# Hashed attention and a SwiGLU block: hash products in four 32-column tiles, a first pair loaded in halves, and a bank of its own for the sums

## The chip, the cores and the metric

The kernel runs on one core of a Trainium2 chip. The metric is the device time of one launch in microseconds (us), median of several runs. "Before" measured 1153.05 us in its first three runs (1152.74 to 1157.72).

PE is TensorE, DVE is VectorE, ACT is ScalarE, POOL is GpSimd and SP is SyncE, which issues most transfers. In profile lines, L248 is line 248 of that kernel's own file, so the same statement has another number in another kernel: hash products are L248 before and L276 (full width) or L285 (packed) after. The names in them: qraw and kraw are the loaded q and k, tps the transposes and qT and kT their copies, hps the hash products, qb and kb the bits, sc the scores, A their exponentials, acc the running sums of A, av the products of A with v, e and r parts of the softmax's division, g and val the two first products of the feed-forward, t and ht what is made of them, words the weights as they arrive.

## The reference, cut to what matters

```python
# q, k, v: (4, 8, 768, 64); proj: (64, 6)
q_bits = einsum('bhsd,dk->bhsk', q, proj) > 0      # 6 bits per row; k_bits alike
mask   = bucket(q_bits)[:, :, :, None] == bucket(k_bits)[:, :, None, :]
attn   = softmax(where(mask, q @ k.T / 8, -1e9))
x      = (attn @ v)                                 # as (3072, 512)
out    = (silu(x @ w_gate) * (x @ w_val)) @ w_out   # 512 -> 1536 -> 512
```

The weights arrive as float64 words and are narrowed to float32 on VectorE.

## The kernel before

Two heads form a pair (128 partitions); 4 batches of 4 pairs make 16. A pair is worked in 12 units (two halves of q, six chunks of k), two units to a loop step. During batch one TensorE has only attention; from batch two on it works the feed-forward of the batch before, cut into "atoms", between the attention steps. Meanwhile the next pair is prepared: q and k are transposed, by TensorE in the first five pairs and by VectorE later, multiplied with the hash weights, and the signs become the bits.

```python
def front_bank(name):                # where transposes and hash products land
    return side_bank(name) if atoms or next(turn) % 3 == 2 else bank(name)
# side_bank: one bank, shared with the softmax sums; bank: two, shared with the feed-forward

def hash_bits(name, half):
    ...
    ps = front_bank("hps")
    nc.tensor.matmul(ps[:, 0:HQ], hash_w[name], T[name, n][:, cols], start=True, stop=True)
    if name == "q":
        nc.scalar.activation(o, ps[:, 0:HQ], AF.Sign, bias=nudge)
    else:
        nc.vector.tensor_scalar(o, ps[:, 0:HQ], scalar1=above_k, scalar2=times_k,
                                op0=ALU.is_gt, op1=ALU.mult)
...
for half in range(2):                # order: q0, k0, q1, k1
    for name in "qk":
        steps.append(lambda name=name, half=half: hash_bits(name, half))
...
# per loop step: two scores, the sums that are due, two attends, then:
while atoms and credit >= 1.0:       # about three atoms
    atoms.pop(0)()
    narrow_on(4)                     # four VectorE instructions on the weights
    if mine: mine.pop(0)()           # a step of the next pair
```

The softmax here doesn't subtract the row's maximum and nothing guards it: scores larger than these inputs give would overflow.

## Time and profile before

| What | Before | How to read it |
|---|---|---|
| time | 1153.05 us | median of runs |
| TensorE busy | 99% | union of its instructions |
| hash products on TensorE | 64, in 128 records | a float32 product is two records, called its two passes here |
| start to start of one hash product | 0.65 us | from the timeline in the second half |
| TensorE idle for VectorE's softmax sums | 5.5 us | all of it in batch one |

The lines that carry this stand in the prediction. The evacuation of the hash products, per instruction (line, operation, out and in, count | busy us, mean ns | idle before and its releaser), in the page of before:

```profile
L253 DVE TENSOR_SCALAR kb<-hps,above_k,times_k 128x384 bf16<-128x384 f32 x32 | 21.6, 674 | 57.7 <-PE hps L248 57.0
L251 ACT ACTIVATE qb<-hps,nudge 128x384 bf16<-128x384 f32 x32 | 18.6, 581 | 61.0 <-PE hps L248 61.0
```

### The profile page before, as it was taken

How to read it: one execution, taken by the hardware profiler on the slowest of the kernel's cores; microseconds unless marked ns; L12 is line 12 of the kernel's file. 1: busy time of each engine (PE TensorE's matmuls, PEld its weight loads, DVE VectorE, ACT ScalarE, POOL GpSimd, SP SyncE). 2: the span in 40 equal slices, each digit the busy share in tenths (PEclk: the TensorE clock that was granted, in tenths of full speed). 3: DMA queues.
4: the chain of work that ended last, by engine and by line, in shares of the span. 5: the costliest groups of instructions: out<-in, count | busy, mean ns of one | idle time of the engine just before them, and what ended most of it. 6: DMA issues, size and time to landing. Idle time of an engine off the chain costs nothing.

```text
span 1152.5 us, 10719 instructions
## 1 busy us (share of the span) xinstructions
PE 1139.5 (99%) x4357; PEld 562.2 (49%) x4357; DVE 527.4 (46%) x783; ACT 260.9 (23%) x397; POOL 19.5 (2%) x46
## 2 busy tenths in 40 slices
PE   8999999999999999999999999999999999999998
PEld 4444455555444455555544445555554445555543
DVE  4898999999931244334432143443433222222100
ACT  4544221211212212222221222222222120101000
POOL 0000000000000000000000000000000000000000
PEclk9999999999999999999999999999999999999999
DMA  6332424223110220200002040010000000000000
GB/s 146 78 96 60 104 79 119 74 98 102 62 33 19 50 37 1 42 1 14 1 12 48 19 81 7 11 31 1 14 1 10 19 19 9 1 1 0 1 28 28
DMA packets 97874, 44.74 MB, mean 39 GB/s; under 512 B 86048, under 2 KB 90144, under 8 KB 97824
## 3 DMA queue, kind: packets, MB, share of 16 engines
q1 hardware_dynamic: 91200, 25.83, 10.0%
q0 software_dynamic: 4896, 17.83, 4.9%
q8 instruction: 34, 0.56, 0.2%
q10 hardware_dynamic: 1728, 0.40, 0.2%
q14 instruction: 16, 0.13, 0.0%
HBM read 37.75 MB, written 6.29 MB: 38 GB/s over the span
## 4 chain that ended last, share of the span: by engine, by line
PE 98%; DVE 1%; DMA 0%; ACT 0%; SPq 0%; issue 0%; ACTq 0%
PE g L341 22%; PE po L362 22%; PE val L341 22%; PE sc L288 14%; PE av L299 11%; PE hps L248 4%; PE sum L320 2%; DVE r L323 1%; PE tps L238 1%; DMA qraw<-in_q_dram 0%; ACT A L290 0%; DVE wv L205 0%; SPq L100 0%; ACT o L366 0%; DVE t L348 0%
## 5 line engine op out<-in xcount | busy, mean ns | idle before, releaser
L341 PE MATMUL val<-xT,wv 128*128 128x384 f32 x768 | 266.1, 489 | 0.3 <-DVE wv L205 0.3
L341 PE MATMUL g<-xT,wg 128*128 128x384 f32 x768 | 265.9, 489 | 0.0
L362 PE MATMUL po<-wo,ht 128*128 128x512 f32 x576 | 255.4, 596 | 0.0
L290 ACT ACTIVATE A<-sc 128x768 f32<-128x768 f32 x192 | 155.4, 813 | 204.0 <-PE sc L288 196.0
L341 PEld LDWEIGHTS val<-xT,wv 128*128 128x128 f32 x768 | 143.9, 190 | 110.5 <-DVE acc L307 6.0
L341 PEld LDWEIGHTS g<-xT,wg 128*128 128x128 f32 x768 | 143.9, 190 | 109.8 <-DVE acc L307 6.0
L362 PEld LDWEIGHTS po<-wo,ht 128*128 128x128 f32 x576 | 107.5, 190 | 138.4 <-issue 134.9
L288 PE MATMUL sc<-qT,kT 64*128 64x384 f32 x768 | 155.1, 482 | 0.0
L323 DVE RECIPROCAL r<-sum 128x384 f32<-128x384 f32 x32 | 81.8, 2557 | 149.4 <-PE sum L320 149.4
L299 PE MATMUL av<-A,vraw 128*64 128x386 f32 x768 | 144.1, 496 | 0.0
L347 ACT ACTIVATE t<-g 128x384 f32<-128x384 f32 x96 | 47.1, 491 | 415.9 <-PE g L341 415.9
L348 DVE SCALAR_TENSOR_TENSOR t<-t,g 128x384 f32<-128x384 f32 x96 | 53.0, 552 | 191.7 <-ACT t L347 191.7
L307 DVE TENSOR_TENSOR acc<-acc,A 128x768 f32<-128x768 f32 x128 | 122.2, 955 | 33.7 <-ACT A L290 28.7
L353 DVE SCALAR_TENSOR_TENSOR ht<-t,val 128x384 f32<-128x384 f32 x96 | 53.0, 552 | 114.3 <-PE val L341 114.3
L299 PEld LDWEIGHTS av<-A,vraw 128*64 128x64 f32 x768 | 49.3, 136 | 81.4 <-issue 80.1
L288 PEld LDWEIGHTS sc<-qT,kT 64*128 64x128 f32 x768 | 68.7, 189 | 21.4 <-issue 21.4
L288 PE MATMUL sc<-qb,kb 64*128 64x384 bf16 x384 | 63.6, 328 | 0.1
L288 PEld LDWEIGHTS <-kb 64*128 64x128 bf16 x384 | 18.7, 93 | 67.9 <-issue 54.6
L366 ACT COPY o<-po 128x512 f32<-128x512 f32 x24 | 14.1, 586 | 159.7 <-PE po L362 159.7
L253 DVE TENSOR_SCALAR kb<-hps,above_k,times_k 128x384 bf16<-128x384 f32 x32 | 21.6, 674 | 57.7 <-PE hps L248 57.0
L251 ACT ACTIVATE qb<-hps,nudge 128x384 bf16<-128x384 f32 x32 | 18.6, 581 | 61.0 <-PE hps L248 61.0
L303 DVE SCALAR_TENSOR_TENSOR acc<-A 128x768 f32<-128x768 f32 x32 | 30.5, 952 | 0.5 <-ACT A L290 0.5
(65 smaller groups left out, 373.7 us busy)
## 6 DMA issues: line engine op xcount, KB each, us to landing
vraw<-in_v_dram SPq DMA_DIRECT2D x16, 384.0 KB, 3.5
words<-in_moe_w_val_dram POOLq DMA_DIRECT2D x12, 512.0 KB, 3.8
words<-in_moe_w_out_dram POOLq DMA_DIRECT2D x12, 512.0 KB, 3.5
out_dram<-o SPq DMA_DIRECT2D x24, 256.0 KB, 2.0
words<-in_moe_w_gate_dram POOLq DMA_DIRECT2D x10, 512.0 KB, 4.0
qraw<-in_q_dram SPq DMA_DIRECT2D x44, 96.0 KB, 3.4
kraw<-in_k_dram SPq DMA_DIRECT2D x44, 96.0 KB, 3.0
qraw<-in_q_dram SPq DMA_DIRECT2D x10, 192.0 KB, 5.4
```

What stands on the lines that cost most here:

```text
L248: nc.tensor.matmul(ps[:, 0:HQ], hash_w[name], T[name, n][:, cols], start=True, stop=True)
L288: nc.tensor.matmul(sc[:, h, 0:HQ], x["k", n][rows, ks], x["q", n][rows, qs], start=start, stop=not start)
L290: nc.scalar.activation(ring[u % RING][:, :, 0:HQ], sc[:, :, 0:HQ], AF.Exp, scale=SCALE)
L299: nc.tensor.matmul(ps[h * D : (h + 1) * D, 0:AW], raws["v", n][:, h, c, :], a[:, h, :], start=c == 0, stop=c == NCH - 1)
L303: nc.vector.scalar_tensor_tensor(out=acc[n, half], in0=ring[(u - 1) % RING][:, :, 0:HQ], scalar=S * EPS / P, in1=a[:, :, 0:HQ], op0=ALU.ad ...
L307: nc.vector.tensor_tensor(acc[n, half], acc[n, half], a[:, :, 0:HQ], op=ALU.add)
L323: nc.vector.reciprocal(r, ps[:, 0:HQ])
L341: nc.tensor.matmul(ps[:, 0:HQ], w[:, j, f * P : (f + 1) * P], x[:, j, half * HQ : (half + 1) * HQ], start=j == 0, stop=j == NJ - 1)
L347: nc.scalar.activation(t, ps[:, 0:HQ], AF.Tanh, scale=0.5)
L348: nc.vector.scalar_tensor_tensor(out=t, in0=t, scalar=1.0, in1=ps[:, 0:HQ], op0=ALU.add, op1=ALU.mult)
L353: nc.vector.scalar_tensor_tensor(out=ht, in0=now["t"], scalar=0.5, in1=ps[:, 0:HQ], op0=ALU.mult, op1=ALU.mult)
L362: nc.tensor.matmul(ps, hs[half][f][:, i * P : (i + 1) * P], wo[:, f, :], start=f == 0, stop=f == NF - 1)
```

## The change

The intent is to cut TensorE's work and its idle time. A hash product needs only 26 of its 128 output columns. With both heads' columns inside one group of 32, the four products of a pair (q and k, two halves each) fit side by side in four 32-column tiles, and land in one bank, 32 partitions each. From the ninth pair on this is done. Each quarter is then copied to two 32-row places by two instructions. The sums keep a bank to themselves in batch one. The first pair's q and k come in halves, so that scores can begin after half of the preparation. Other edits come with it: q and k have one raw buffer instead of two, the second pair's loads go behind the first weights, and the second halves are hashed in the order k, q instead of q, k.

```diff
 def front_bank(name):
-    return side_bank(name) if atoms or next(turn) % 3 == 2 else bank(name)
+    return side_bank(name) if atoms else bank(name)

+def hash_blocks():
+    ps = front_bank("hps")
+    where = [(name, half) for name in "kq" for half in range(2)]
+    for i, (name, half) in enumerate(where):
+        nc.tensor.matmul(ps[i * BLOCK : (i + 1) * BLOCK, 0:HQ], hash_w[name][:, 0:BLOCK],
+                         T[name, n][:, half * HQ : (half + 1) * HQ], start=True, stop=True)
+    for i, (name, half) in enumerate(where):
+        for to in (0, D):
+            sign(name, half, slice(to, to + BLOCK), ps, slice(i * BLOCK, (i + 1) * BLOCK))
 ...
-for half in range(2):
-    for name in "qk":
-        steps.append(lambda name=name, half=half: hash_bits(name, half))
+if n >= 2 * NP:
+    return steps + [hash_blocks]
+order = [("q", 0), ("k", 0), ("k", 1), ("q", 1)]
+# first pair: q0 k0 before the first score, then k1, then q1, each transposed and hashed
 ...
-load(0, nc.scalar)                    # whole q, k, v; two raw buffers
+fetch(0, "q", nc.sync, 0)             # first half of q; one raw buffer for q and for k
+fetch(0, "k", nc.scalar, 0)
+fetch(0, "k", nc.sync, 1)
+fetch(0, "v", nc.sync)
+fetch(0, "q", nc.sync, 1)
 ...
-load(1)                               # then the first two pieces of the weights
+load_words(0, nc.sync); load_words(1, nc.sync); load(1)
-    if at == 0 and n + 1 < len(pairs):
+    if at == (4 if n == 0 else 0) and n + 1 < len(pairs):
```

(Cut: the set-up of the hash weights and of the three constant columns, which follows the new layout.)

More of the change, by code (lines that the diff above doesn't have):

```diff
@@ L79, with fetch @@
     raws = {}
-    def load(n, k_queue=nc.sync):
+    def fetch(n, name, queue, half=None):
         b, pr = pairs[n]
-        for name, src, queue in (("q", q, nc.sync), ("k", k, k_queue)):
-            t = raw.tile([P, NCH, 2, D], FP32, tag=name + "raw", name=name + "raw")
-            if n > NP:
-                blocks = t.rearrange("p c a b -> p (c a b)").rearrange(
-                    "p (c a d) -> p c a d", a=P // BLOCK, d=BLOCK)
-                for h in range(2):
-                    for x in range(D // BLOCK):
-                        at = h * D + x * BLOCK
-                        queue.dma_start(
-                            blocks[at : at + BLOCK],
-                            src[b, 2 * pr + h][:, x * BLOCK : (x + 1) * BLOCK].rearrange(
-                                "(a p c) d -> p c a d", c=NCH, p=BLOCK))
-                raws[name, n] = t
-                continue
-            for h in range(2):
-                queue.dma_start(t[:, :, h, :],
-                                  src[b, 2 * pr + h].rearrange("(p c) d -> p c d", c=NCH))
-            raws[name, n] = t
-        t = raw.tile([P, 2, NCH, D], FP32, tag="vraw", name="vraw")
-        nc.sync.dma_start(
-            t.rearrange("p h c d -> p h (c d)"),
-            v[b, 2 * pr : 2 * pr + 2].rearrange("h (p c) d -> p h (c d)", c=NCH),
-        )
-        raws["v", n] = t
@@ L110 @@
-    load(0, nc.scalar)
+        if name == "v":
+            t = raws["v", n] = raw.tile([P, 2, NCH, D], FP32, tag="vraw", name="vraw")
+            queue.dma_start(
+                t.rearrange("p h c d -> p h (c d)"),
+                v[b, 2 * pr : 2 * pr + 2].rearrange("h (p c) d -> p h (c d)", c=NCH),
+            )
+            return
+        src = q if name == "q" else k
+        if not half:
+            raws[name, n] = raw.tile([P, NCH, 2, D], FP32, tag=name + "raw", name=name + "raw",
+                                     bufs=1)
@@ new lines, in fetch @@
+        t = raws[name, n]
+        if n <= NP:
+            cs = slice(None) if half is None else slice(half * CH, (half + 1) * CH)
+            for h in range(2):
+                queue.dma_start(t[:, cs, h, :],
+                                src[b, 2 * pr + h].rearrange("(p c) d -> p c d", c=NCH)[:, cs, :])
+            return
+        blocks = t.rearrange("p c a b -> p (c a b)").rearrange(
+            "p (c a d) -> p c a d", a=P // BLOCK, d=BLOCK)
+        for h in range(2):
+            for x in range(D // BLOCK):
+                at = h * D + x * BLOCK
+                queue.dma_start(
+                    blocks[at : at + BLOCK],
+                    src[b, 2 * pr + h][:, x * BLOCK : (x + 1) * BLOCK].rearrange(
+                        "(a p c) d -> p c a d", c=NCH, p=BLOCK))
@@ L112, with load @@
+    def load(n):
+        for name in "qkv":
+            fetch(n, name, nc.sync)
+    two_proj = konst.tile([P, NBITS], FP32, tag="proj", name="proj")
+    for o in (0, D):
+        nc.gpsimd.dma_start(two_proj[o : o + D, :], proj[:, :])
+    fetch(0, "q", nc.sync, 0)
[3 more added lines that the diff above has]
+    fetch(0, "q", nc.sync, 1)
     ident = konst.tile([P, P], FP32, tag="ident", name="ident")
@@ L120 @@
         nc.tensor.matmul(ps, zeros[:, 0:P], zeros, start=True, stop=True)
-    two_proj = konst.tile([P, NBITS], FP32, tag="proj", name="proj")
-    for o in (0, D):
-        nc.scalar.dma_start(two_proj[o : o + D, :], proj[:, :])
+    HR = 16
+    assert 2 * NBITS + 1 <= HR and 2 * HR == BLOCK
+    rules = konst.tile([P, 3, P], FP32, tag="rules", name="rules")
+    nc.gpsimd.memset(rules[:, 0, :], -(2.0**-120))
+    nc.gpsimd.memset(rules[:, 1:3, :], 0.0)
+    groups = rules.rearrange("p x (g r) -> p x g r", r=HR)
+    nc.gpsimd.memset(groups[:, 0, :, 2 * NBITS : 2 * NBITS + 1], 1.0)
+    nc.gpsimd.memset(groups[:, 1, :, NBITS : 2 * NBITS + 1], -1.0)
+    for h in range(2):
+        g = groups[:, 2, h * D // HR + h, :]
+        nc.gpsimd.memset(g[:, 0:NBITS], OFF)
+        nc.gpsimd.memset(g[:, NBITS : 2 * NBITS], -OFF / 2)
+        nc.gpsimd.memset(g[:, 2 * NBITS : 2 * NBITS + 1], -NBITS * OFF / 2)
+    nc.vector.tensor_tensor(rules, rules, ident.unsqueeze(1).to_broadcast([P, 3, P]), op=ALU.mult)
+    columns = konst.tile([P, 3], FP32, tag="columns", name="columns")
+    nc.vector.tensor_reduce(out=columns, in_=rules, axis=AX.X, op=ALU.add)
+    nudge, above_k, times_k = (columns[:, x : x + 1] for x in range(3))
     hash_w = {}
@@ L130 @@
         hash_w[name] = konst.tile([P, P], FP32, tag="hash" + name, name="hash" + name)
-        nc.gpsimd.memset(hash_w[name], 0.0)
-    def column(name, first, second, third, rest):
-        t = konst.tile([P, 1], FP32, tag=name, name=name)
-        nc.vector.memset(t, rest)
-        for o in (0, D):
-            nc.vector.memset(t[o : o + 2 * NBITS + 1], third)
-            nc.vector.memset(t[o : o + 2 * NBITS], second)
-            nc.vector.memset(t[o : o + NBITS], first)
-        return t
-    nudge = column("nudge", -1e-37, -1e-37, 1.0, -1e-37)
-    above_k = column("above_k", 0.0, -1.0, -1.0, 0.0)
-    times_k = column("times_k", OFF, -OFF / 2, -NBITS * OFF / 2, 0.0)
-    ones = konst.tile([P, D], FP32, tag="ones", name="ones")
-    nc.vector.memset(ones, 1.0)
-    for name in "qk":
-        for o in (0, D):
-            for at in (0, NBITS) if name == "q" else (0,):
-                nc.vector.tensor_copy(hash_w[name][o : o + D, o + at : o + at + NBITS],
-                                      two_proj[o : o + D, :])
+        nc.vector.memset(hash_w[name], 0.0)
+        for h in range(2):
+            rows = slice(h * D, (h + 1) * D)
+            for at in (0, NBITS) if name == "q" else (0,):
+                at += h * HR
+                nc.vector.tensor_copy(hash_w[name][rows, at : at + NBITS], two_proj[rows, :])
+        nc.vector.tensor_copy(hash_w[name][:, D : D + BLOCK], hash_w[name][:, 0:BLOCK])
+    sides = {}
+    for name in "qk":
+        for i in range(2):
+            sides[name, i] = konst.tile([P, S], BF16, tag=name + f"b{i}", name=name + "b")
+    ones = konst.tile([P, D], FP32, tag="ones", name="ones")
+    nc.gpsimd.memset(ones, 1.0)
     RING = 4
@@ L214, in narrow_on @@
             next(narrowing, None)
-    for i in range(2):
-        load_words(i, nc.sync)
+    load_words(0, nc.sync)
+    load_words(1, nc.sync)
+    load(1)
     T = {}
@@ L222 @@
     atoms = []
-    turn = iter(range(1 << 20))
     def front_bank(name):
-        return side_bank(name) if atoms or next(turn) % 3 == 2 else bank(name)
+        return side_bank(name) if atoms else bank(name)
     def front(n):
         def transpose(name, half):
-            if half == 0:
+            if (name, n) not in T:
                 T[name, n] = opnd.tile([P, S], FP32, tag=name + "T", name=name + "T")
@@ L241, in transpose, with sign @@
             nc.scalar.copy(T[name, n][:, half * HQ : (half + 1) * HQ], ps[:, 0:HQ])
+        bits["q", n] = sides["q", n % 2]
+        bits["k", n] = sides["k", n % 2]
+        def sign(name, half, to, ps, at):
+            o = bits[name, n][to, half * HQ : (half + 1) * HQ]
+            if name == "q":
+                nc.scalar.activation(o, ps[at, 0:HQ], AF.Sign, bias=nudge[to])
+            else:
+                nc.vector.tensor_scalar(o, ps[at, 0:HQ], scalar1=above_k[to], scalar2=times_k[to],
+                                        op0=ALU.is_gt, op1=ALU.mult)
         def hash_bits(name, half):
-            if half == 0:
-                bits[name, n] = opnd.tile([P, S], BF16, tag=name + "b", name=name + "b")
-            cols = slice(half * HQ, (half + 1) * HQ)
             ps = front_bank("hps")
-            nc.tensor.matmul(ps[:, 0:HQ], hash_w[name], T[name, n][:, cols], start=True, stop=True)
-            o = bits[name, n][:, cols]
-            if name == "q":
-                nc.scalar.activation(o, ps[:, 0:HQ], AF.Sign, bias=nudge)
-            else:
-                nc.vector.tensor_scalar(o, ps[:, 0:HQ], scalar1=above_k, scalar2=times_k,
-                                        op0=ALU.is_gt, op1=ALU.mult)
+            nc.tensor.matmul(ps[:, 0:HQ], hash_w[name], T[name, n][:, half * HQ : (half + 1) * HQ],
+                             start=True, stop=True)
+            sign(name, half, slice(0, P), ps, slice(0, P))
+        def hash_blocks():
[7 more added lines that the diff above has]
+                    sign(name, half, slice(to, to + BLOCK), ps, slice(i * BLOCK, (i + 1) * BLOCK))
         def transpose_blocks(name):
@@ L264, in front @@
                 steps.append(lambda name=name: transpose_blocks(name))
-        else:
-            for half in range(2):
-                for name in "qk":
-                    steps.append(lambda name=name, half=half: transpose(name, half))
-        for half in range(2):
-            for name in "qk":
-                steps.append(lambda name=name, half=half: hash_bits(name, half))
+        if n >= 2 * NP:
+            return steps + [hash_blocks]
+        order = [("q", 0), ("k", 0), ("k", 1), ("q", 1)]
+        for at in (order[0:2], order[2:3], order[3:4]) if n == 0 else (order,):
+            if n <= NP:
+                for x in at:
+                    steps.append(lambda x=x: transpose(*x))
+            for x in at:
+                steps.append(lambda x=x: hash_bits(*x))
         return steps
@@ L377, in push_ffn @@
                     atoms.append(lambda half=half, i=i, f=f: down(half, i, range(f, f + 3)))
-    for step in front(0):
-        step()
+    steps = front(0)
+    for _ in range(4):
+        steps.pop(0)()
     N = len(units)
@@ L387 @@
     credit = 0.0
-    steps = []
     left = []
@@ L406 @@
         left = [u, u + 1]
-        mine = [steps.pop(0) for _ in range(2) if u % per >= 2 and steps]
+        mine = [steps.pop(0) for _ in range(2) if (u < 4 or u % per >= 2) and steps]
         if not atoms:
```

## The prediction

> **What bounds the kernel now.** I read the page's engine shares first, then the chain that ended last, then the groups of the operations that the change touches, then the waits of TensorE, and last TensorE's timeline at the places where these stand.
>
> ```profile
> PE 1139.5 (99%) x4357; PEld 562.2 (49%) x4357; DVE 527.4 (46%) x783; ACT 260.9 (23%) x397; POOL 19.5 (2%) x46
> ...
> PE 98%; DVE 1%; DMA 0%; ACT 0%; SPq 0%; issue 0%; ACTq 0%
> ```
>
> TensorE (PE) is busy for 1139.5 of 1152.5 us and is 98% of the chain. So the time can fall in two ways only: TensorE's own work shrinks, or the 13 us in which it idles do.
>
> ```profile
> L248 PE MATMUL hps<-qT,hashq 128*128 128x384 f32 x64 | 27.3, 508 | 2.7 <-DVE e L325 2.7
> L248 PE MATMUL hps<-kT,hashk 128*128 128x384 f32 x64 | 26.0, 488 | 0.5 <-DVE e L325 0.5
> ...
> PE hps L248 <- DVE e L325: 3.2, 3, 1.4
> PE tps L238 <- DVE e L325: 2.3, 2, 1.4
> PE tps L238 <- DMA qraw<-in_q_dram: 1.7, 1, 1.7
> PE idle L120 <- DVE nudge L134: 1.2, 1, 1.2
> PE val L341 <- DVE wv L205: 0.3, 1, 0.3
> ```
>
> The groups give the hash products 53.3 us in all; one float32 product is two records (16 pairs x 2 names x 2 halves = 64 products, 128 records). The list of TensorE's waits gives idle time, times and the longest: 5.5 us in five waits for the end of a softmax sum's evaluation on VectorE (e, L325), 1.7 us for the first q, and 1.2 us of launch. That is nearly all the idle time there is.
>
> ```profile
> 498.07 0.81 PE L248 MATMUL hps<-qT,hashq 128*128 128x384 f32 x2
> 498.72 2.74 PE L341 MATMUL val<-xT,wv 128*128 128x384 f32 x8
> 501.30 0.81 PE L248 MATMUL hps<-kT,hashk 128*128 128x384 f32 x2
> 501.94 2.74 PE L341 MATMUL g<-xT,wg 128*128 128x384 f32 x8
> ```
>
> TensorE's timeline (start, duration, instruction) in the second half: a hash product stands between two feed-forward steps of the same 128*128 tile. Its printed 0.81 us overlaps the next one; start to start it costs 498.72 - 498.07 = 0.65 us. A feed-forward step costs 501.30 - 498.72 = 2.58 us, four products of 0.645.
>
> ```profile
> 480.64 0.81 PE L288 MATMUL sc<-qT,kT 64*128 64x384 f32 x4
> 481.29 0.33 PE L288 MATMUL sc<-qb,kb 64*128 64x384 bf16 x2
> 481.45 0.81 PE L288 MATMUL sc<-qT,kT 64*128 64x384 f32 x4
> 482.19 0.87 PE L320 MATMUL sum<-acc,ones 128*64 128x384 f32 x4
> 482.88 1.47 PE L299 MATMUL av<-A,vraw 128*64 128x386 f32 x8
> 484.28 2.85 PE L341 MATMUL val<-xT,wv 128*128 128x384 f32 x8
> 486.96 2.74 PE L341 MATMUL g<-xT,wg 128*128 128x384 f32 x8
> ```
>
> Here the tile changes three times. The sums are two products in two 64-column tiles, and both together take 482.88 - 482.19 = 0.69 us, hardly more than one. So column tiles do run at once here, in float32 and each with its own moving data. A change of tile is dear only by tenths: the step after av takes 486.96 - 484.28 = 2.68, 0.10 more than 2.58. The eight av records take 1.40 against four passes of about 0.32, that is 0.10 more.
>
> **What the skill says.** (1) "TensorEngine Tiling (Array Packing)", section Key Properties: changing the tiling mode drains TensorE, while different tiles load weights and multiply in parallel. The trace agrees with both, with the 0.1 us and the 0.69 us above. (2) "TensorE: Matmul & The Clock Gate", Part 3, the measured speedup against the span model: the span of packed products is one product's duration plus about 4 ns per further tile, and three 32-column tiles measured 2.38 times. The trace shows two tiles only; four in float32 is what no line of it shows. (3) Tiling page, section PSUM Bottleneck: tiling speeds up TensorE, not the evacuation. The change even doubles the evacuating instructions, see below. (4) Clock gate page, Part 1: TensorE starts at half clock until it has been busy for about 3.4 us. The first transposes in the trace take 0.66 us for three, from 6.91 to 7.57, and 0.43 later (97.61 to 98.04), so the start is still cold although nine idle products ran from 1.19 to 5.2.
>
> **The change, part by part.**
>
> Hash products. For the last eight pairs, four products of 128*128 (4 x 0.645 = 2.58 us) become four of 128*32 side by side in one bank. If they run at once: 0.645 for two passes. They stand after the first feed-forward step of an iteration, between 128*128 products, so two changes of tile come in that were not there before. In: the first sum record starts about 0.41 after the last score record where 0.32 is the step, +0.09, and its own first pass is about 0.05 longer because its weights weren't loaded ahead. Out: the same about +0.09 at the border, and +0.10 in the step that follows. Sum 0.645 + 0.33 = 0.98 us; saved 2.58 - 0.98 = 1.60 per pair, 8 x 1.60 = 12.8 us, all on TensorE's path. The other eight pairs keep their full-width products and save nothing.
>
> Evacuation of these. A half's bits go to two 32-row places, so there are four Sign on ScalarE and four comparisons on VectorE per pair instead of two and two. With 581 and 675 ns each (the rows of qb and kb, whose time I take to follow the 384 columns and not the partitions) that is 1.2 us more on ScalarE and 1.35 us more on VectorE per pair. Both have room in this half: from 320 to 400 us VectorE is busy for 19.3 of 80 us and ScalarE for 16.9. A burst of 2.3 to 2.7 us delays the evacuation of the feed-forward's two banks, but each step in between lasts 2.58 us and a bank is wanted again two steps later, so I count 0.
>
> The sums' own bank in batch one. Before, every third front product took the bank that the sums use; now these use the other two, which nothing else takes before the feed-forward starts. That removes the reason for the 5.5 us. I don't count all of it, because VectorE is nearly full there:
>
> ```profile
> core 0: us, PE busy (x) PEld busy (x) DVE busy (x) ACT busy (x) POOL busy (x), PEclk, DMA share, GB/s
> ...
> 30.00:60.00 30.00, 27.23 (x159) 11.67 (x155) 25.90 (x34) 14.22 (x21) 1.05 (x2) 1.00 0.35 93
> 60.00:90.00 30.00, 30.00 (x180) 13.35 (x182) 27.92 (x38) 15.15 (x23) 1.05 (x2) 1.00 0.28 76
> 90.00:123.50 33.50, 30.77 (x184) 13.11 (x180) 29.22 (x39) 17.15 (x25) 1.05 (x2) 1.00 0.37 84
> ```
>
> VectorE is busy for 83.0 of 93.5 us in these three stretches. With TensorE's 5.5 us gone, 83.0 in 88.0 is 94%. It fits if the ring of four attention tiles absorbs the lag after each reciprocal (2.56 us, then 0.6 for xT). I count three quarters, 4.1 us.
>
> The start. q and k of the first pair come in halves, and scores begin after two transposes and two hash products instead of four and four. The first q half should land about when the idle products end, at 5.3 instead of 6.9 us: the issue of two transfers (1.65 us for whole ones, I take somewhat less) is shorter and half the bytes are ahead of it. From 5.3: transposes cold to 6.6, hash to about 8.7, comparison to 9.5, then the first score, against 12.72 before. But about 3.2 us of the work before that score is only moved behind it: the second halves' transposes and products now stand between scores, each with a wait for the copy that separates a transpose from its product (0.48 us and the hand-over, say 0.6, twice). Worked forward, the second half of q is hashed at about 17.9, where the kernel before stands at 17.79 with the same work done. Moreover q and k have one raw buffer instead of two: the second pair's transfers wait for the last transposes of the first pair (about 16 us), and two transfers of 192 KB need 5.4 us (q) and 6.2 us (k) to land, so the second pair's first transposes at about 21 us may find k missing for a microsecond. Against that, the clock may warm sooner without the 1.7 us gap. I count 0.5 us gained, give or take 1.5. The set-up work (rules and columns on GpSimd and VectorE in place of 21 memsets of 0.06 us) ends before it is needed unless the transfer of proj, now issued by GpSimd, lands late (5.0 us before).
>
> Sum: 12.8 + 4.1 + 0.5 = 17.4 us off 1153.05, 1135.6 us, 1.5%.
>
> **Rivals.** (a) Four float32 column tiles don't all run at once. If only two do, a block costs 1.29 + 0.33 = 1.62, saves 0.96 and 7.7 us in all, and the time is about 1140.7. If none do, each block is 2.58 + 0.33, the change costs 2.6 us there, and the time is about 1151. For it: the trace has no four-tile line, and each tile brings its own stream of moving data. Against it: two tiles cost nothing extra (0.69). I give two at a time 12% and none at once 6%. (b) VectorE becomes the bound of batch one, since it stands at 89% there: a wait for the attention tile's sum (acc) through ScalarE's exponential takes the place of the wait for e, and only 1 or 2 of the 5.5 us come back; 1138 us. For it: ScalarE already waits there for acc, 3.6 us in three waits. Against it: VectorE waited 12.3 us for hash products between 12 and 124 us, slack that moves forward when TensorE does. 25%. (c) The start loses instead of gaining, through the single raw buffer: up to 2 us more, 1137.5. 35%. (d) The doubled evacuation stalls the feed-forward's banks: at most about 1 us per pair, 8 us, 1143.5. 7%.
>
> **Range and chances.** The three terms together save at most about 13.9 + 5.5 + 2.5 = 21.9 us (13.9 if only a border of 0.1 on each side is paid), 1131.2. The limit of 2% is 1130.0, so faster by more needs something that I haven't seen: 5%. Rivals b and c together end near 1140, rival a with one of them near 1143. My range is 1131.5 to 1142.5. Slower by 2% would need 40 us of new waits: 1%.
>
> **What would show it.** The hash rows of the last eight pairs: eight records of one block starting four by four, and about 0.65 us from the first to the end of the second pass; the next feed-forward step about 0.98 us after the block's start. If the starts come two by two or one by one, rival a. TensorE's waits for e from 30 to 124 us: gone, with little for other VectorE work in their place; if ScalarE's waits for acc grow to several us, rival b. The first score near 9.5 us and the second pair's kT transposes without a wait over 1 us; otherwise rival c. ScalarE's Sign at about 0.58 us on 32 partitions; if it were shorter, the evacuation would be cheaper than I count, with no effect on the time. Wrong by more than the range would mean that the hash block is not what I take it for.

## The result, and the profile after

The kernel after takes 1139.16 us (1139.05 to 1139.7 in four runs) against 1153.66 in the same rounds. The ratio is 0.987, with a 95% interval of 0.984 to 0.989: faster by 1.3%, within 2%. Ratios are the mean time of one kernel's fast runs over that of the other's fast runs of the same rounds, so they are not quite the ratio of the medians quoted.

From the page of the kernel after, the engines and the chain:

```profile
PE 1126.2 (99%) x4357; PEld 548.9 (48%) x4357; DVE 538.4 (47%) x783; ACT 269.1 (24%) x413; POOL 21.0 (2%) x57
...
PE 96%; DVE 3%; ACT 0%; DMA 0%; issue 0%; SPq 0%; DVEq 0%; ACTq 0%
```

TensorE still sets the end, and 13.3 us of its busy time are gone. Its waits in the kernel after (waiting instruction, releaser: us, times, longest):

```profile
PE hps L276 <- DVE kb L271: 1.7, 2, 1.1
PE tps L258 <- DMA kraw<-in_k_dram: 1.2, 1, 1.2
PE idle L134 <- DVE zeros L131: 1.2, 1, 1.2
PE hps L276 <- ACT qT L261: 0.8, 2, 0.6
PE hps L276 <- ACT kT L261: 0.8, 1, 0.8
PE sc L325 <- DVE kb L271: 0.8, 1, 0.8
```

The waits for e are gone, but others have come: hps for kb, transposes for k's transfer, and three kinds for the first pair's copies and bits. Where the time went is best seen by milestones. The table has the start of the first av record of a pair, counted from one, as I read it from the traces of both kernels:

| Milestone | Before, us | After, us | Difference |
|---|---|---|---|
| pair 1 | 16.34 | 14.11 | -2.23 |
| pair 2 | 42.71 | 42.39 | -0.32 |
| pair 3 | 69.50 | 67.56 | -1.94 |
| pair 5 (end of batch one) | 122.16 | 117.49 | -4.66 |
| pair 8 | 336.79 | 334.79 | -2.00 |
| pair 9 | 404.64 | 401.04 | -3.60 |
| pair 16 | 900.42 | 885.62 | -14.79 |
| end | 1152.53 | 1137.42 | -15.11 |

From pair 8 on the difference grows by 1.60 us with every pair: 12.8 us in eight. That is the packed block, which the timeline of TensorE in the kernel after shows between two atoms:

```profile
490.19 2.85 PE L378 MATMUL g<-xT,wg 128*128 128x384 f32 x8
492.97 0.52 PE L285 MATMUL hps<-kT,hashk 128*32 128x384 f32 x2
492.98 0.52 PE L285 MATMUL hps<-qT,hashq 128*32 128x384 f32 x2
493.31 0.49 PE L285 MATMUL hps<-kT,hashk 128*32 128x384 f32 x2
493.33 0.49 PE L285 MATMUL hps<-qT,hashq 128*32 128x384 f32 x2
493.75 2.85 PE L378 MATMUL val<-xT,wv 128*128 128x384 f32 x8
496.43 2.74 PE L378 MATMUL g<-xT,wg 128*128 128x384 f32 x8
```

The four first passes start together and the four second passes follow 0.34 us later; the next atom starts 493.75 - 492.97 = 0.78 us after the block. That atom takes 2.68 us instead of 2.58, and the last step of the one ahead is already lengthened by the border (2.78, of which 0.10 is its own first pass after av). So a block costs 0.98 us in the place of four times 0.645.

But between pairs 5 and 8 the kernel after *loses* 2.66 us, and nothing in the prediction says so. Here is the place, first in the timeline of all engines in the kernel after, then TensorE in the kernel before:

```profile
145.65 0.81 PE L276 MATMUL hps<-kT,hashk 128*128 128x384 f32 x2
146.29 2.74 PE L378 MATMUL val<-xT,wv 128*128 128x384 f32 x8
...
148.30 0.43 DVE L219 TENSOR_SCALAR words<-words 128x512 int32<-128x512 int32 x1
148.76 0.69 DVE L222 CUSTOM_DVE_ANT_0 wg<-words,wg 128x1024 uint16<-128x1024 uint16 x1
149.37 0.67 DVE L271 TENSOR_SCALAR kb<-hps,columns 128x384 bf16<-128x384 f32 x1
...
150.10 0.91 PE L276 MATMUL hps<-qT,hashq 128*128 128x384 f32 x2 [1.06 <-DVE kb L271]
```

```profile
150.31 0.81 PE L248 MATMUL hps<-qT,hashq 128*128 128x384 f32 x2
150.95 2.74 PE L341 MATMUL val<-xT,wv 128*128 128x384 f32 x8
...
153.53 0.81 PE L248 MATMUL hps<-kT,hashk 128*128 128x384 f32 x2
```

From batch two on both products of such a step share the one side bank, so the second must wait until the first is evacuated. Before, q came first and the lightly used ScalarE freed the bank. After, k comes first, and VectorE reaches its comparison only behind the four narrowing instructions of the atom: at 149.37, when the bank was filled at about 146.5. TensorE idles for 1.06 us.

The start is mixed. The first score comes at 8.44 instead of 12.72 us, but the lead of 2.23 us at pair 1 is 0.32 at pair 2, although a wait of 1.36 us for e, which the kernel before has in that stretch, is gone. So apart from the sums' bank the start lost 1.0 us. TensorE's timeline of the kernel after:

```profile
8.44 0.34 PE L325 MATMUL sc<-qb,kb 64*128 64x384 bf16 x2 [0.77 <-DVE kb L271]
...
11.51 0.91 PE L276 MATMUL hps<-kT,hashk 128*128 128x384 f32 x2 [0.81 <-ACT kT L261]
...
16.67 0.91 PE L276 MATMUL hps<-qT,hashq 128*128 128x384 f32 x2 [0.57 <-ACT qT L261]
...
22.43 0.52 PE L258 MATMUL tps<-ident,kraw 128*128 128x128 f32 x3 [1.20 <-DMA kraw<-in_k_dram]
```

The first three waits (2.15 us together) are those of a short chain (transpose, copy, product, bits) with nothing beside it; the last is the second pair's k.

### The profile page after: what moved, and what is told of

It reads as the page before. It is cut to its first block, busy times and chain, and to the rows that moved or that the text cites. A ratio compares the mean times of both kernels' runs of the same rounds, so it can differ in the third digit from the quotient of the medians.

```text
span 1137.4 us, 10768 instructions
## 1 busy us (share of the span) xinstructions
PE 1126.2 (99%) x4357; PEld 548.9 (48%) x4357; DVE 538.4 (47%) x783; ACT 269.1 (24%) x413; POOL 21.0 (2%) x57
## 4 chain that ended last, share of the span: by engine, by line
PE 96%; DVE 3%; ACT 0%; DMA 0%; issue 0%; SPq 0%; DVEq 0%; ACTq 0%
PE po L399 22%; PE g L378 22%; PE val L378 22%; PE sc L325 13%; PE av L336 11%; PE sum L357 2%; PE hps L276 2%; DVE acc L344 1%; PE tps L258 1%; PE hps L285 1%; DVE r L360 0%; DMA kraw<-in_k_dram 0%; PE idle L134 0%; DVE kb L271 0%; DVE wv L226 0%
## 5 line engine op out<-in xcount | busy, mean ns | idle before, releaser
L269 ACT ACTIVATE qb<-hps,columns 32x384 bf16<-32x384 f32 (+1 forms) x48 | 27.7, 577 | 77.3 <-DVE kb L271 44.6
L271 DVE TENSOR_SCALAR kb<-hps,columns 32x384 bf16<-32x384 f32 (+1 forms) x48 | 32.1, 669 | 24.2 <-PE hps L285 17.2
```

The lines of the kernel that those rows point to most:

```text
L271: nc.vector.tensor_scalar(o, ps[at, 0:HQ], scalar1=above_k[to], scalar2=times_k[to], op0=ALU.is_gt, op1=ALU.mult)
```

## The experiments

Twelve kernels ran, each beside runs of the kernel before on the same chip; all gave correct results. "After" is 1139.16 us throughout. The 95% intervals of the ratios are about 0.0015 to either side, most of it from the kernel before (1152.7 to 1156.0 in these rounds), while the runs of one new kernel mostly lie within 0.8 us. So I compare medians and, for differences under 2 us, the milestones of the traces.

**1. The order of the second halves (e1_order).**

```diff
 order = [("q", 0), ("k", 0), ("k", 1), ("q", 1)]
+if n > NP:
+    order = [("q", 0), ("k", 0), ("q", 1), ("k", 1)]
```

> One line changed in the kernel after: pairs six to eight hash the second half of q before the second half of k, as the kernel before did. Theory O (the 2.66 us that the kernel after loses against before between the fifth and the eighth pair come from the new order, in which a product evacuated by the loaded VectorE stands just ahead of the next one in the same single bank): TensorE's waits of hps for kb in that stretch (1.7 us) go, and the time is 2.4 to 2.7 us below the kernel after, about 1136.6. Rival D (VectorE is simply short of time there, whatever the order): the wait moves to another instruction, and the time is within 0.8 us of the kernel after, 1138.4 to 1140.

Measured 1136.40 us (ratio 0.9854), 2.76 below the kernel after. Its lead over before is 4.81 us at pair 5 and still 4.81 at pair 8, and the wait of hps for kb is gone from the list. Theory O holds; rival D falls.

**2. Nothing packed (e2_no_pack).**

```diff
-if n >= 2 * NP:
+if n >= 99:
     return steps + [hash_blocks]
```

> The kernel after, with full-width hash products in all pairs (nothing packed). Theory H (packing is worth 1.60 us in each of eight pairs): 12.8 us above the kernel after, 1152.0, at most a microsecond more from waits of the kind that the new order of halves brings (then about 1152.5). Rival: packing also relieves the evacuation or the single bank, and taking it away costs clearly more, over 15 us (1154 and up).

Measured 1152.21 us (0.9990), 13.05 above the kernel after. From pair 8 to pair 16 its difference to the kernel before stays at 1.85 to 1.84 us. Packing is worth what theory H says, and the other parts of the change together come to 1.2 us by the ratio (whose interval, 0.9973 to 1.0007, includes no gain at all) and 1.85 us in the traces.

**3. The sums' bank shared again in batch one (e3_old_bank).**

```diff
-return side_bank(name) if atoms else bank(name)
+return side_bank(name) if atoms or next(turn) % 3 == 2 else bank(name)
```

> The kernel after, with every third front product of batch one in the sums' bank again. Theory B (the own bank gave back the whole 5.7 us that lie in the intervals with waits for e): TensorE waits for e again in batch one, and the time is 4.5 to 6 us above the kernel after, 1143.7 to 1145.2. Rival V (VectorE bounds batch one, so the waits only change their name): under 2.5 us above, below 1141.7.

Measured 1143.69 us (0.9916), 4.5 above the kernel after. The waits are back in the list:

```profile
PE tps L259 <- DVE e L363: 2.2, 2, 1.4
PE hps L277 <- DVE e L363: 1.9, 2, 1.4
```

Theory B holds for the cause: with the bank shared, 4.5 us are lost again, and VectorE, though 93% busy there in the kernel after (82.8 of 88.8 us), does not take its place. The size is at the expected lower edge. The wait of 1.36 us that the kernel before has in its first pair doesn't come back with the new start.

**4. The old start (e4_old_start).**

```diff
-fetch(0, "q", nc.sync, 0); fetch(0, "k", nc.scalar, 0); ...   # halves
+fetch(0, "q", nc.sync); fetch(0, "k", nc.scalar); fetch(0, "v", nc.sync)
-for _ in range(4):           # steps before the first score
+for _ in range(8):
-load_words(0); load_words(1); load(1)      # and bufs=1
+load(1); load_words(0); load_words(1)      # and bufs=2
```

(Abridged: the first pair's steps also take their old order, the second pair's preparation starts in the first pair's second step as before, and the constants' rules share another buffer.)

> The kernel after, with the start of before: q and k of the first pair whole, four transposes and four hash products before the first score, two raw buffers, the second pair's loads early, its transposes in the first pair's second step (the set-up of the constants stays as in the kernel after, its rules only lie in another buffer). Theory S (the new start loses 1.0 us against the old one): 0.7 to 1.6 us below the kernel after, 1137.6 to 1138.5. Rival G (the new start gains, and what the first two pairs show against it is only work moved): 0.3 to 2 us above, 1139.5 to 1141.2.

Measured 1138.25 us (0.9870), 0.9 below the kernel after, with a wide spread (1137.4 to 1139.45) that reaches into the range of the kernel after. Theory S holds by the median; in the profiled run, its fastest, the old start is 1.56 us ahead at pair 2. The spread has a visible candidate. The first transposes stand at the same place in both traces, first the kernel before, then this one:

```profile
6.91 0.87 PE L238 MATMUL tps<-ident,qraw 128*128 128x128 f32 x3 [1.70 <-DMA qraw<-in_q_dram]
7.57 0.85 PE L238 MATMUL tps<-ident,kraw 128*128 128x128 f32 x3
```

```profile
6.89 0.52 PE L256 MATMUL tps<-ident,qraw 128*128 128x128 f32 x3 [1.69 <-DMA qraw<-in_q_dram]
7.25 0.49 PE L256 MATMUL tps<-ident,kraw 128*128 128x128 f32 x3
```

Three transposes take 0.66 us there and 0.36 here, after the same idle products and the same gap of 1.7 us: TensorE was still at its slow clock in one execution and at full speed in the other. (The clock records kept with the traces begin with the full clock at 10.6 us in the first and at 5.9 us in the second.) So the loss of 1.0 us at pair 2 that was read above is against a kernel before with a slow first 10 us; against this warm trace of the old start it is 1.56. This agrees with the Trainium skill, page "TensorE: Matmul & The Clock Gate", Part 1, which says that the window of the clock gate runs freely, so that the moment of warming varies from run to run. In the kernel after the gap is gone and the transposes were warm. That the four runs' spread comes from this is only argued: I have one trace of each kernel.

**5. Two raw buffers (e5_two_raw).**

```diff
-raws[name, n] = raw.tile([P, NCH, 2, D], FP32, tag=name + "raw", name=name + "raw", bufs=1)
+raws[name, n] = raw.tile([P, NCH, 2, D], FP32, tag=name + "raw", name=name + "raw")
-rules = konst.tile([P, 3, P], FP32, tag="rules", name="rules")
+rules = (a view of one of the acc buffers, which are idle then)
```

> The kernel after with two raw buffers for q and k, as before (the constants' rules share another buffer, to make room); all else as in the kernel after, the second pair's loads still last in the queue. Theory R (the second pair's transposes find k missing for 1.2 us because its transfer waits for the single raw buffer): TensorE's wait of tps for kraw goes, and the time is 1.0 to 1.4 us below the kernel after, 1137.8 to 1138.2. Rival Q (k is late because of its place behind the weights in the queue): the wait stays, the time is within 0.4 us of the kernel after.

Measured 1137.90 us (0.9863), 1.26 below the kernel after; 0.98 us ahead at pair 2 and constant from there. The wait for kraw is gone. Theory R holds: the single buffer, not the place in the queue, made k late.

**6. Packed from the sixth pair on (e6_pack_from_6th).**

```diff
-if n >= 2 * NP:
+if n >= NP + 1:
     return steps + [hash_blocks]
```

> The kernel after with packed hash products from the sixth pair on instead of the ninth. Theory P (TensorE's path alone decides, and the evacuation has room): three more pairs save 1.6 us each and the 2.7 us of the order's waits go with them, 7.5 us below the kernel after, 1131.7. Rival E (VectorE, 93% busy in that stretch, cannot take 1.35 us more per pair): a wait of the feed-forward or of the sums for VectorE appears, and at least a third of the 7.5 us is missing, 1134.2 or more.

Measured 1139.48 us (0.9883; 1138.99 to 1142.38): no gain at all, against the 7.5 us of theory P. A new wait stands first in TensorE's list:

```profile
PE g L378 <- DVE t L385: 4.4, 3, 1.9
```

Theory P falls for these pairs; rival E holds so far, but which part of the evacuation is to blame is not told by it. One thing more is in the profiled run: after the longest of these waits the granted clock was 0.50 from 223.42 to 226.83 us, and the feed-forward step in it (start 222.31) took 4.36 us to the next start instead of 2.68. The clock isn't the whole cause: one of the four runs has a mean clock of 1.000 and still took 1139.22 us; the slowest, 1142.38, has 0.997.

**7. Packed from the third pair on (e7_pack_from_3rd).**

```diff
 for x in at:
     steps.append(lambda x=x: transpose(*x))
+if n >= 2:
+    steps.append(hash_blocks)
+    continue
```

> As the run with packing from the sixth pair, and also in the third to fifth pair, where the transposes are TensorE's and VectorE is busy for 94%. Theory P: 2.0 us less in each of three more pairs (two groups of 1.49 us become a block of 0.98), 6 us below the run from the sixth pair. Rival E: VectorE is the bound there, a wait for acc or kb takes the place, and under 3 us of the 6 arrive.

Measured 1144.27 us (0.9917), 5.1 slower than the kernel after and 4.8 slower than the run before it. None of the 6 us arrives. TensorE now waits in batch one for the exponential:

```profile
PE sc L328 <- ACT A L330: 7.4, 3, 2.6
PE g L381 <- DVE t L388: 4.5, 3, 1.9
```

The size is past rival E's, and the wait is another than the two it names. The trace tells two causes. At each of the three places the exponentials start just when the four Signs end (58.58 us after Signs from 56.22 for 2.33; likewise 84.31 and 111.16), and these had waited for the comparisons (9.9 us in three times). So the trace places the 7.4 us in ScalarE's queue, which runs 8 and 10 below are about; late Signs were not tried in these pairs, so that stays argued. And the granted clock was 0.50 for 3.41 us three times, each after a wait of 1.9 to 2.4 us (from 85.28, 112.59 and 228.64 us; a wait of 2.6 us at 59 us had no such sequel); run 6 has one of these. Half speed for 3.41 us costs about 1.7 us, an estimate, so the two in batch one cost 3.4. With the 7.4 that is 10.8 us: the 6.0 that weren't gained and the 4.8 that were lost. All four runs have a mean clock of 0.996 or 0.997.

**8. The block ahead of the first atom (e8_block_first).**

```diff
+if n + 1 >= 2 * NP and u % per == 4:
+    for step in mine: step()
+    mine = []
 credit += rate
 while atoms and credit >= 1.0:
```

> The kernel after, with the packed block ahead of the first feed-forward step of its iteration instead of behind it, so that it lies next to av, where the tile changes anyway. Theory T (a change of tile costs TensorE 0.1 to 0.2 us each, as the sum of the prediction has it): one change fewer in each of eight pairs, 0.8 to 1.6 us below the kernel after, 1137.6 to 1138.4. Rival: the cost is the block's own (the first pass of 0.34 us and weights), and nothing changes, 1139.0 to 1139.5.

Measured 1141.53 us (0.9896), 2.4 *above* the kernel after, so both expectations missed the total. The milestones take it apart: against the kernel after, five of the eight blocks gain 0.20 us each and three lose 1.08 each. The 0.20 is the change of tile that theory T asks for. The loss is seen in the timeline of one of the three:

```profile
490.70 2.85 PE L378 MATMUL g<-xT,wg 128*128 128x384 f32 x8
490.84 2.72 DVE L271 TENSOR_SCALAR kb<-hps,columns 32x384 bf16<-32x384 f32 x4 [1.57 <-PE hps L285]
493.39 2.74 PE L378 MATMUL val<-xT,wv 128*128 128x384 f32 x8
493.65 2.33 ACT L269 ACTIVATE qb<-hps,columns 32x384 bf16<-32x384 f32 x4 [4.19 <-DVE kb L271]
496.01 0.49 ACT L384 ACTIVATE t<-g 128x384 f32<-128x384 f32 x1
...
497.15 1.24 PE L378 MATMUL g<-xT,wg 128*128 128x384 f32 x3 [1.02 <-DVE t L385]
```

The four comparisons and the four Signs read different quarters of one bank, yet the Signs start only when the comparisons end (493.65): the built program makes ScalarE wait for VectorE there, in all eight blocks. The evacuation takes not 2.7 us but 5.1, and the tanh of g, whose product is done at about 493.5, stands behind the Signs in ScalarE's queue until 496.01. Then g's bank comes free too late for the next g.

**9. Both repairs together (e9_order_raw)**: the edits of runs 1 and 5.

> The kernel after with both mended parts: q ahead of k in the second halves of pairs six to eight (2.8 us in its own run) and two raw buffers (1.0 to 1.3 us in its own run). If the two are independent the time is 3.8 to 4.1 us below the kernel after, 1135.1 to 1135.4; if the gain of one is taken by VectorE, which both make busier in the same stretch, under 3.3 us arrive, above 1135.8.

Measured 1135.52 us (0.9841), 3.64 below the kernel after. It falls between the two bands, but in the trace the gain is 3.59 us, of which 0.93 is there at pair 2 and the other 2.65 come between pairs 5 and 8, so they are independent.

**10. The Signs one atom later (e10_late_signs)**: run 9, the block ahead of the first atom, and

```diff
-return steps + [hash_blocks]
+signs("k"); later.append(lambda: signs("q"))      # inside hash_blocks
+return steps + [hash_blocks, lambda: later.pop()()]
```

> The kernel of the run before in this call, with the packed block ahead of the first feed-forward step (as in the run that moved the block there and lost), but ScalarE's four Sign instructions issued one feed-forward step later than the block. Theory W (there the loss of 3 us came from the Signs, which wait for VectorE's comparisons of the same bank and hold the tanh of the next step behind them in ScalarE's queue): no stall of g for t is left, each of eight pairs saves 0.2 us, 1.6 us below the run before, about 1133.6. Rival X (the evacuation is simply too long, 5 us, wherever it stands): TensorE's waits of g for t stay at 2 us or more, and the time isn't below the run before.

Measured 1133.61 us (0.9826), 1.9 below run 9 (1.97 in the traces, of which 0.39 is there before the first block and 1.58 comes from the eight blocks, 0.20 each). No wait of g for t is left. The same place as above, now without a stall:

```profile
489.28 2.74 PE L386 MATMUL val<-xT,wv 128*128 128x384 f32 x8
489.48 0.49 ACT L392 ACTIVATE t<-g 128x384 f32<-128x384 f32 x1 [4.12 <-DVE kb L271]
489.99 2.33 ACT L269 ACTIVATE qb<-hps,columns 32x384 bf16<-32x384 f32 x4
...
491.86 2.75 PE L386 MATMUL g<-xT,wg 128*128 128x384 f32 x8
```

Theory W holds: the order in ScalarE's queue was the cause, not the length of the evacuation.

**11. The same from the sixth pair on (e11_late_6th)**: the condition of run 6 in run 10.

> The same with late Signs, and packed from the sixth pair on, where packing gained nothing in its first run. Theory W (that run's 4.4 us of waits of g for t had the same cause, the order in ScalarE's queue): three more pairs save 1.8 us each, 5.3 us below the run with late Signs from the ninth pair, about 1128.3. Rival E (VectorE, 93% busy there, hasn't the time for 1.35 us more per pair and for a comparison in four pieces): waits for VectorE of 3 us or more stay, 1131.5 or more.

Measured 1132.60 us (0.9817, interval 0.9803 to 0.9832), 1.0 below run 10. Of the 5.3 us of theory W, 1.0 arrives. 3.5 us of waits for VectorE stand in the three pairs:

```profile
PE val L384 <- DVE ht L396: 2.0, 2, 1.5
PE g L384 <- DVE t L391: 1.5, 1, 1.5
```

The time lies in rival E's band. Between pairs 5 and 8 run 6 takes 218.0 us, run 10, which packs nothing there, 214.6, and run 11 213.7 (starts of av in the traces). So late Signs and the moved block together gave 4.4 us back in that stretch, of which about 1.7, an estimate from the step of 4.36 us, is the half-speed clock that run 6's trace has there and run 11's has not. Rival E's waits keep most of the rest.

**12. Less narrowing beside the block (e12_less_narrow)**: run 11, and

```diff
-narrow_on(4)
+narrow_on({4: 2, 6: 5, 10: 5}.get(u % per, 4) if u // per in (NP, NP + 1, NP + 2) else 4)
```

> The run packed from the sixth pair with late Signs, and in the step of those three pairs in which the block stands, VectorE narrows the weights in two instructions per feed-forward step instead of four, made up by five instead of four in two later steps of the pair. Theory L (the 3.5 us of waits that were left there, of val and g for VectorE's ht and t, are a burst: the comparison's 2.7 us on top of the narrowing in one step): they go, 3.5 to 4.2 us below that run, about 1128.6. Rival E (VectorE lacks the time over the whole stretch): the waits move to the later steps, and the time is within 1.5 us of that run, 1131.1 or more.

Measured 1136.38 us (0.9846), 3.8 *above* run 11. TensorE's waits grew:

```profile
PE val L384 <- DVE ht L396: 3.9, 4, 1.7
PE g L384 <- DVE t L391: 1.5, 1, 1.5
...
PE hps L285 <- DVE kT L299: 0.8, 2, 0.5
```

Theory L falls. Work pushed into later steps makes new waits there (at 160 and 232 us), and those beside the block stay. This fits rival E's picture of a VectorE without slack, but it lost even more than the rival expected. What exactly holds VectorE up beside the block stays open.

## Why the prediction was right or wrong

Class and range were right; the point was 3.6 us too fast, 17.4 us of gain against 14.5 (the kernel before measured 0.6 us more in the later rounds). That it came so close is partly luck: against the 14.8 us found below, the errors of the bank (+1.6) and the start (-1.5) nearly cancel, and what is left is a step that the prediction didn't have. By its own steps:

- **Hash products (12.8 predicted).** Exact: 1.60 us per block in the milestones, 12.8 in eight, 13.05 by taking the packing out. The working holds in its parts too: 0.98 us per block, and 0.20 us for one border between tiles (runs 8 and 10). Rival (a) fell, since all four tiles start within 0.02 us.
- **Evacuation (0 predicted).** 0 in the kernel after, as every block saved its full 1.60 us. One step of the working was wrong all the same: "a burst of 2.3 to 2.7 us" took the two engines to work side by side. They work in series, 5.1 us, and rival (d) was one moved block away (run 8). That an instruction's time follows the columns and not the partitions was right: 668 ns on 32 partitions against 675 on 128 on VectorE, 574 against 581 on ScalarE.
- **The sums' bank (4.1 predicted).** 4.5 when taken back in run 3; between the two kernels it is 5.7, namely the first pair's wait of 1.36 and 1.62 + 2.72 from the milestones of the stretches with the other waits. I had cut the 5.5 us to three quarters for VectorE's load, and that cut was too much, by 0.4 us after run 3 and by 1.6 after the traces. ScalarE did wait longer for acc, as rival (b) has it (10.6 us from 12 to 124 us, 3.6 before), but TensorE lost nothing by that.
- **The start (0.5 us gain predicted, give or take 1.5).** The sign was wrong: it lost 1.0 us against the kernel before, and 0.9 against the old start in run 4. The prediction names the cause among its doubts, k missing for "a microsecond" because of the single raw buffer (rival c). The wait was 1.2 us and run 5 gives 1.0 to 1.3 us back. It weighed a warm clock against that. The clock was warm, and with the first pair's preparation done the kernel after is 0.27 us ahead (its next scores start at 17.52, the next work of the kernel before at 17.79), better than the 0.1 behind to which the chain was worked forward. So the term that failed is the wait for k, which the 0.5 left almost uncounted.
- **The order of halves (not in the sum).** This is the step that was missing. The part "The other eight pairs keep their full-width products and save nothing" passed over that their order changes. It cost 2.7 us (run 1), which is most of the miss.

The sum of what was found, 12.8 + 5.7 - 1.0 - 2.7 = 14.8 us, compares with 15.1 between the two traces and 14.5 between the medians. One reading of the prediction was too generous: the waits that it calls nearly all of TensorE's idle time are 8.7 of 13.0 us; the other 4.3 lie behind its last product.

## What to carry to other kernels

Small products that fill a quarter of the columns can share the array where TensorE sets the time: here four took 0.98 us in place of 2.58, changes of tile included. The price is an evacuation that needs room in the queues of the other engines. When two products share one bank, put first the one whose evacuating engine is idle, and look in a diff for changes of order as carefully as for changes of work. Before an instruction that waits for another engine goes into a queue, ask what comes behind it: moving four Signs by one step turned a loss of 2.4 us into a gain of 1.6.

## What the Trainium skill lacked or had wrong

- "TensorEngine Tiling (Array Packing)", Key Properties: it says that a change of tiling mode drains TensorE, without a figure. Here a border between tiles costs about 0.1 us plus about 0.1 us in the first pass behind it, and taking one border away saved 0.20 us in each of eight places.
- "TensorE: Matmul & The Clock Gate", Part 3: its measured speedups have three column tiles, and no type is named. Here four float32 tiles, each with its own moving data, start within 0.02 us and take 0.78 us to the next instruction, where four full-width products take 2.58.
- "TensorEngine Tiling (Array Packing)", PSUM Bottleneck: it advises to use ScalarE and VectorE both for the evacuation. That section gives no figure for the case that the built program makes the two take turns on one bank, even on different quarters of it: here 2.72 us and then 2.33 us, 5.1 in all.
